# Block-sparse attention and a gated MLP on one core: the mask of 36 of 44 block pairs by eight products of 32 columns instead of two of 128

## The chip, the cores and the metric

The kernel runs on one core of one Trainium2 chip. The metric is the device time of one execution in microseconds. The engines named below are TensorE (PE, its weight loads shown apart as PEld), VectorE (DVE), ScalarE (ACT), GpSimd (POOL) and SyncE (SP).

## What is computed

Attention over 4 batches, 8 heads, 768 positions and a head size of 64, with a mask in blocks of 32 positions (24 blocks). A block of queries sees its neighbours, the first and the last block, and three sampled blocks; the first and the last block of queries see everything. The result goes through an MLP with 512 inputs, 2048 hidden units and 512 outputs.

```python
scores = scale * np.matmul(q, k.transpose(0, 1, 3, 2))
mask = np.abs(blk_i - blk_j) <= window
mask = mask | (blk_i == 0) | (blk_j == 0) | (blk_i == n_blocks - 1) | (blk_j == n_blocks - 1)
for qb in range(n_blocks):
    for kb in sampled_blocks[qb]:
        mask[qb * block:(qb + 1) * block, kb * block:(kb + 1) * block] = True
scores = np.where(mask, scores, -1000000000.0)
...
attn = attn / (np.sum(attn, axis=-1, keepdims=True) + 1e-09)
...
h = x @ w_in
g = h * (1.0 / (1.0 + np.exp(-beta * h)))
return (g @ w_out).astype(np.float32)
```

## The kernel before

The 22 inner query blocks of a batch are taken two at a time, which makes 11 pairs a batch and 44 pairs in all, numbered n = 0 to 43; p is the number within the batch. For a pair the kernel gathers eight key blocks for each of its two query blocks (three sampled, one and three fixed, one) into the tile KG, so that a row has 8 x 32 = 256 scores. The same sampled block can stand in the gathered row more than once, or beside a neighbour that is there already; such doubles are masked.

The scores of a pair lie in two PSUM banks, one for each head of a head pair (u = 0, 1). A bank holds 128 rows (four head pairs hp of 32 queries) by 512 columns (two query blocks g of 256). They are made by two steps that follow each other on PE:

- emit_sm, lines 810 to 818, writes the mask: a product of a constant tile `ones` (64 rows, 128 columns) with a small row of mask numbers `maskr`, spread over 32 columns a block. It covers `ns` = 3 blocks of each query block (192 columns in all), or 5 blocks (320 columns) for the first and the last pair of a batch (p = 0 and p = 10). One product for each bank, so two a pair. Each works on a PE tile of 64 rows by 128 columns.
- emit_ss, lines 820 to 830, adds the scores: sixteen products for a pair (g, hp, u), each on a PE tile of 64 rows by 32 columns, with 256 columns moving.

From pair 33 on, two pairs share one step of the order (lines 831 to 843): both masks first, then both sets of scores. These double steps are the pairs 34 and 35, 36 and 37, 38 and 39, 40 and 41, 42 and 43.

After that DVE takes the row maximum (L848), ACT the exponential (L856), DVE or POOL normalizes (L881), PE transposes (L895), ACT or DVE copies the transposes (L304, L306), and PE multiplies by V (L936, or L944 for the early pairs). The rows of the first and the last query block go through steps of their own (L1000 to L1063), and with 64x32 PE tiles for their scores (L1000). The MLP's products are L1129 (into the hidden layer, followed by a tanh on ACT at L1135 and a product on DVE at L1140) and L1156 (out of it). They are put between the attention steps all along.

The order of all steps is written out by hand in a long string ORDER; each engine runs its own steps in that order, and semaphores hold a step until its inputs are there. A step named sc7 in that string is the mask and the scores of pair 7, and a number behind a colon names PSUM banks. The string is the same for both kernels. Where it has two sc steps one behind the other (sc0, sc2 and sc1, for instance), PE goes from the scores of one pair straight to the mask of the next.

Of the kernel before, what the change touches and what calls it, by code (L numbers as in the profile page):

```python
# [192 lines left out]
def kernel(  # L193
# [11 lines left out]
    nc = tc.nc  # L205

    B, H, S, D = q.shape
    BLK = 32
# [3 lines left out]
    NHP = H // 2  # L212
# [12 lines left out]
    def sb(name, shape, dt=FP16):  # L225
        return pool.tile(shape, dt, name=name)
# [10 lines left out]
    NLATE, PTA, ODS, AHEAD = 11, 0.9, 0.8, 3  # L237
    NHOT, NV = 0, 2
    NHL, UP, NH32 = 4, 1024.0, 7

    by_dma = lambda n: n >= TD[0] and n % TD[1] < TD[2]
    TD = (31, 1, 1)
# [18 lines left out]
    ones = sb("ones", [P, P])  # L261
    maskr = sb("maskr", [P, NB - 2, 5])
# [389 lines left out]
    for n, (b, p) in enumerate(order_pairs):  # L652
# [157 lines left out]
        def emit_sm(n=n, p=p):  # L810
            bk = [bank(("S", n, u)) for u in range(2)]
            ns = 5 if p in (0, NPAIR - 1) else 3
            for u in range(2):
                nc.tensor.matmul(  # L814
                    bk[u][:, :].rearrange("x (g c) -> x g c", g=2)[:, :, 0:ns * BLK],
                    lhsT=ones[u * D:(u + 1) * D, :],
                    rhs=maskr[u * D:(u + 1) * D, 2 * p:2 * p + 2, 0:ns].to_broadcast([D, 2, ns, BLK]),
                    start=True, stop=False, skip_group_check=True, tile_position=(u * D, 0))

        def emit_ss(n=n, b=b, i0=i0, kgb=kgb):  # L820
            bk = [bank(("S", n, u)) for u in range(2)]
# [11 lines left out]
        if two == [n - 1]:  # L833

            t = sc[n] = sc[n - 1]
            t.deps += [d for d in sdeps if d not in t.deps]
            t.opens += (("S", n, 0), ("S", n, 1))
            t.ni *= 2
            halves[n - 1] += [emit_sm, emit_ss]
        else:  # L840
            halves[n] = [emit_sm, emit_ss]
            sc[n] = add(f"sc{n}", "PE", 0.62 if two else 0.31, lambda h=halves[n]: [f() for f in h[0::2] + h[1::2]],
                        deps=sdeps, prio=pr, lat=0.1, opens=(("S", n, 0), ("S", n, 1)))
# [388 lines left out]
```

## Time and profile before

| | us |
|---|---|
| median of 3 runs | 298.3 (297.95 to 299.88) |
| the profiled execution | 298.2 |
| its span, first to last instruction | 296.3 |
| PE busy | 277.1 |
| DVE busy | 227.2 |
| ACT busy | 220.4 |
| POOL busy | 170.1 |

The profile is of one execution. A row of the timeline or of the groups names an engine, a line of the kernel, the operation, what it writes and reads, the PE tile (rows x columns, written 64\*32), the size of the moving operand, and a count. The ends of products are modelled, so that a busy PE may be waiting for its own pipeline; what a product really costs is read from the starts. "Idle" is time in which an engine had nothing running.

### The profile page before, as it was taken

Reading aid. Unit: us, or ns where it says so; the run is one execution under the profiler, and the core shown is the slowest. Engines: PE = TensorE matmul, PEld = TensorE weight load, DVE = VectorE, ACT = ScalarE, POOL = GpSimd, SP = SyncE. Lnnn points to the kernel's source line nnn. Section 1 sums busy time; section 2 is a strip of 40 time slices with the busy share of each in tenths; the row PEclk is TensorE's granted clock in tenths of the full one; section 3 lists DMA queues with packets and bytes.
Section 4 is the critical chain, followed back from the end, with each engine's and each line's share of the span. In section 5 each row is a group of like instructions: output and inputs, shape, how many; then the busy total and the mean of one; then the engine's idle time right before and its main releaser. Section 6 shows DMA issues by size and latency. Waiting matters only on the chain.

```text
span 296.3 us, 10828 instructions
## 1 busy us (share of the span) xinstructions
PE 277.1 (94%) x3841; PEld 173.1 (58%) x3841; DVE 227.2 (77%) x538; ACT 220.4 (74%) x644; POOL 170.1 (57%) x508
## 2 busy tenths in 40 slices
PE   1599999898999999999999999999999999999993
PEld 0455768667577577655656665555455455557641
DVE  5879889987999899899998999787867642575420
ACT  3328989889999798979989989768758644855630
POOL 3058986316898997878777788748545606000000
PEclk9999999999999999999999999999999999999998
DMA  7999999999966745936973256355654554630203
GB/s 246 366 310 200 227 236 229 220 210 212 196 108 146 162 130 194 200 107 114 241 161 107 78 163 223 85 118 132 124 158 94 169 121 146 175 89 0 73 35 106
DMA packets 57168, 47.51 MB, mean 160 GB/s; under 512 B 19734, under 2 KB 53143, under 8 KB 57115
## 3 DMA queue, kind: packets, MB, share of 16 engines
q1 hardware_dynamic: 44736, 35.48, 41.8%
q0 software_dynamic: 12320, 11.27, 24.7%
q8 instruction: 30, 0.49, 0.7%
q14 instruction: 24, 0.19, 0.2%
q10 hardware_dynamic: 58, 0.07, 0.1%
HBM read 45.23 MB, written 9.44 MB: 184 GB/s over the span
## 4 chain that ended last, share of the span: by engine, by line
PE 69%; ACT 11%; DVE 11%; DMA 3%; issue 3%; SPq 0%; POOL 0%; DVEq 0%; ACTq 0%
PE bank L1156 24%; PE bank L1129 22%; ACT PP L856 5%; PE bank L936 4%; PE bank L791 4%; PE bank L825 4%; PE bank L895 3%; DVE g L1140 3%; DMA g<-in_k_dram 3%; PE bank L593 2%; ACT t L1135 2%; PE bank L814 2%; DVE ST L848 1%; ACT PG L1023 1%; PE bank L1043 1%
## 5 line engine op out<-in xcount | busy, mean ns | idle before, releaser
L1129 PE MATMUL bank<-xT,w_in_sb 128*128 128x256 f16 (+1 forms) x512 | 93.7, 326 | 1.0 <-DVE xT L960 0.4
L856 ACT ACTIVATE PP<-bank,ST 128x256 f16<-128x256 f32 x176 | 82.0, 484 | 16.2 <-DVE ST L848 7.6
L1156 PE MATMUL bank<-w_out_sb,g 128*128 128x512 f16 x384 | 90.6, 379 | 0.7 <-DVE xT L306 0.6
L1140 DVE SCALAR_TENSOR_TENSOR g<-t,bank 128x512 f16<-128x512 f16 (+1 forms) x128 | 67.1, 548 | 25.2 <-ACT t L1135 24.4
L1135 ACT ACTIVATE t<-bank,beta_sb 128x512 f16<-128x512 f32 (+1 forms) x128 | 70.9, 591 | 19.9 <-PE bank L1129 11.3
L881 POOL TENSOR_SCALAR PP<-PP,ST 128x256 f16<-128x256 f16 x132 | 63.7, 500 | 29.6 <-ACT PP L856 10.2
L1129 PEld LDWEIGHTS <-w_in_sb 128*128 128x128 f16 x512 | 54.5, 114 | 27.7 <-issue 3.8
L676 POOL COPY KG<-KT 128x64 f32 x264 | 52.4, 247 | 23.7 <-ACT KT L304 11.4
L848 DVE TENSOR_REDUCE ST<-bank 128x2 f32<-128x512 f32 x88 | 58.1, 681 | 5.8 <-PE bank L825 4.6
L1156 PEld LDWEIGHTS <-g 128*128 128x128 f16 x384 | 36.0, 98 | 39.8 <-issue 2.6
L856 ACT ACTIVATION_READ_ACCUMULATOR PP<-bank,ST 128x1 f32 x176 | 37.8, 215 | 0.0
L1035 POOL TENSOR_SCALAR PG<-PG,SG 128x768 f16<-128x768 f16 x14 | 12.6, 903 | 18.8 <-ACT t L1135 7.7
L310 ACT ACTIVATE osb<-bank 128x512 f32<-128x512 f32 (+1 forms) x24 | 14.0, 595 | 10.9 <-PE bank L1156 10.6
L1023 ACT ACTIVATE PG<-bank,SG 128x384 f16<-128x384 f32 x32 | 18.2, 583 | 2.4 <-DVE SG L1016 2.1
L936 PEld LDWEIGHTS <-VG 128*128 128x128 f16 x448 | 16.1, 98 | 5.0 <-issue 1.1
L895 PE MATMUL bank<-identity,PP 128*128 128x128 f16 x248 | 18.6, 219 | 0.4 <-ACT PP L856 0.2
L306 POOL COPY KG<-KT 128x384 f32<-128x384 f32 (+3 forms) x44 | 17.3, 419 | 1.7 <-PE bank L825 1.7
L895 PEld LDWEIGHTS <-PP 128*128 128x128 f16 x248 | 15.5, 98 | 4.6 <-issue 1.7
L306 DVE COPY PT<-bank 128x1024 f16<-128x1024 f16 x24 | 16.3, 682 | 1.8 <-PE bank L895 1.1
L306 DVE CAST xT<-bank 64x256 f16<-64x256 f32 (+1 forms) x33 | 13.6, 415 | 5.2 <-PE bank L936 4.7
L936 PE MATMUL bank<-PT,VG 128*128 128x64 f16 x448 | 17.2, 193 | 0.2 <-ACT PP L856 0.2
L825 PE MATMUL bank<-KG,QT 64*32 64x256 f16 x704 | 17.2, 274 | 0.0
(114 smaller groups left out, 304.4 us busy)
## 6 DMA issues: line engine op xcount, KB each, us to landing
VG<-VT SPq DMA_DIRECT2D x220, 32.0 KB, 2.2
VG<-VT SPq DMA_DIRECT2D x32, 192.0 KB, 2.8
out_dram<-osb SPq DMA_DIRECT2D x20, 256.0 KB, 2.3
RQ<-in_q_dram POOLq DMA_DIRECT2D x6, 384.0 KB, 9.2
RK<-in_k_dram POOLq DMA_DIRECT2D x6, 384.0 KB, 8.5
RV<-in_v_dram POOLq DMA_DIRECT2D x6, 384.0 KB, 8.6
VT<-Vn SPq DMA_DIRECT2D x3, 768.0 KB, 3.8
w_in_sb<-in_moe_w_in_dram POOLq DMA_DIRECT2D x8, 256.0 KB, 7.5
```

The costliest lines, as they stand in the source:

```text
L306: (nc.vector if eng == "DVE" else nc.gpsimd).tensor_copy(out=out, in_=in_)
L676: nc.gpsimd.tensor_copy(out=kg32[:, g, :, (SR + r) * W:(SR + r + 1) * W], in_=kt32[:, :, bass.ds(vals[3 * g + r], W)])
L825: nc.tensor.matmul(bk[u][hp * BLK:(hp + 1) * BLK, g * 256:(g + 1) * 256], lhsT=QT[b % 2][u * D:(u + 1) * D, hp, (i0 + g) * BLK:(i0 + g + 1 ...
L848: mx[n, u] = add(f"mx{n}.{u}", "DVE", 0.6, lambda n=n, u=u, sb_=sb_: nc.vector.tensor_reduce(out=sb_[:, 0, 2 * u:2 * u + 2], in_=bank(("S" ...
L856: nc.scalar.activation(out=pb[:, u, g, :], in_=bank(("S", n, u))[:, g * 256:(g + 1) * 256], func=AF.Exp, bias=sb_[:, 0, 2 * u + g:2 * u + ...
L881: (nc.vector if eng == "DVE" else nc.gpsimd).tensor_scalar(out=pb[:, u, g, :], in0=pb[:, u, g, :], scalar1=sb_[:, 2, 2 * u + g:2 * u + g + ...
L895: nc.tensor.transpose(out=o[:, s * P:(s + 1) * P], in_=pb[:, u, g, c * P:(c + 1) * P], identity=identity)
L936: nc.tensor.matmul(o[:, (g * NHP + hp) * 2 * BLK:(g * NHP + hp + 1) * 2 * BLK], lhsT=vgb[:, g, c, hp * P:(hp + 1) * P], rhs=pt[:, g, c, :, ...
L1129: nc.tensor.matmul(o[:, 0:TW], lhsT=w_in_v[:, c, f // 4, f % 4, :], rhs=xT[:, c, c0:c0 + TW], start=(c == 0), stop=(c == NHP - 1))
L1135: lambda G=G, f=f, TW=TW, tt=tt: nc.scalar.activation(out=tt[:, 0:TW], in_=bank(("H", G, f))[:, 0:TW], func=AF.Tanh, bias=0.0, scale=beta_ ...
L1140: lambda G=G, f=f, TW=TW, tt=tt, gg=gg: nc.vector.scalar_tensor_tensor(out=gg[:, f, 0:TW], in0=tt[:, 0:TW], scalar=1.0, in1=bank(("H", G, ...
L1156: nc.tensor.matmul(o[:, :], lhsT=gg[:, f, s * P:(s + 1) * P], rhs=w_out_sb[:, f, :], start=(f == 0), stop=(f == N_FFC - 1))
```

## The change

A set FEW names the pairs 3 to 10. For these the mask is written as before, by two products of 128 output columns. For all other pairs it is written by eight products with 32 output columns each, one for each head pair and bank, on the same 64x32 PE tiles and in the same hp, u order as the scores that follow. They read the same `maskr` and a part of the same `ones`, so the numbers that land in PSUM are the same.

```diff
+    FEW = range(3, 11)
...
-            for u in range(2):
-                nc.tensor.matmul(
-                    bk[u][:, :].rearrange("x (g c) -> x g c", g=2)[:, :, 0:ns * BLK],
-                    lhsT=ones[u * D:(u + 1) * D, :],
-                    rhs=maskr[u * D:(u + 1) * D, 2 * p:2 * p + 2, 0:ns].to_broadcast([D, 2, ns, BLK]),
-                    start=True, stop=False, skip_group_check=True, tile_position=(u * D, 0))
+            if n in FEW:
+                for u in range(2):
...
+                return
+            for hp in range(NHP):
+                for u in range(2):
+                    nc.tensor.matmul(
+                        bk[u][hp * BLK:(hp + 1) * BLK, :].rearrange(
+                            "x (g c) -> x g c", g=2)[:, :, 0:ns * BLK],
+                        lhsT=ones[u * D:(u + 1) * D, 0:BLK],
+                        rhs=maskr[u * D:(u + 1) * D, 2 * p:2 * p + 2, 0:ns].to_broadcast([D, 2, ns, BLK]),
+                        start=True, stop=False, skip_group_check=True,
+                        tile_position=(u * D, hp * BLK))
```

PE's instructions grow from 7572 to 8004: 36 pairs by six more products, each with its weight load. Leaving the mask aside, the order and the waits on every engine are the same in both kernels.

On PE, at the first pair of the kernel (n = 0), where its mask ends and its scores begin; the banks are numbered 122 and 124. Before:

```order
L814 LDWEIGHTS ones
L814 MATMUL bank_122<-maskr,ones 128x2x160
L814 LDWEIGHTS ones
L814 MATMUL bank_124<-maskr,ones 128x2x160
L825 LDWEIGHTS QT_74
L825 MATMUL bank_122<-KG_81,QT_74 32x256
L825 LDWEIGHTS QT_74
L825 MATMUL bank_124<-KG_81,QT_74 32x256
```

On PE at the same place, now (line 824 is the narrow mask, 837 the scores); the last two of the eight products are shown:

```order
L824 LDWEIGHTS ones
L824 MATMUL bank_122<-maskr,ones 32x2x160
L824 LDWEIGHTS ones
L824 MATMUL bank_124<-maskr,ones 32x2x160
L837 LDWEIGHTS QT_74
L837 MATMUL bank_122<-KG_81,QT_74 32x256
L837 LDWEIGHTS QT_74
L837 MATMUL bank_124<-KG_81,QT_74 32x256
```

The first number of a size is the count of output rows: 128 before, 32 now, so that mask and scores have the same PE tile.

On PE, where the scores of pair 0 end and the mask of the next pair in the order (n = 2) begins. Before:

```order
L825 LDWEIGHTS QT_74
L825 MATMUL bank_122<-KG_81,QT_74 32x256
L825 LDWEIGHTS QT_74
L825 MATMUL bank_124<-KG_81,QT_74 32x256
L814 LDWEIGHTS ones
L814 MATMUL bank_123<-maskr,ones 128x2x96
L814 LDWEIGHTS ones
L814 MATMUL bank_121<-maskr,ones 128x2x96
```

On PE at the same place, now:

```order
L837 LDWEIGHTS QT_74
L837 MATMUL bank_122<-KG_81,QT_74 32x256
L837 LDWEIGHTS QT_74
L837 MATMUL bank_124<-KG_81,QT_74 32x256
L824 LDWEIGHTS ones
L824 MATMUL bank_123<-maskr,ones 32x2x96
L824 LDWEIGHTS ones
L824 MATMUL bank_121<-maskr,ones 32x2x96
```

Here too the size of the tile no longer changes, where the mask follows on another pair's scores.

More of the change, by code (lines that the diff above doesn't have):

```diff
@@ L812, in emit_sm @@
             ns = 5 if p in (0, NPAIR - 1) else 3
-            for u in range(2):
-                nc.tensor.matmul(
-                    bk[u][:, :].rearrange("x (g c) -> x g c", g=2)[:, :, 0:ns * BLK],
-                    lhsT=ones[u * D:(u + 1) * D, :],
-                    rhs=maskr[u * D:(u + 1) * D, 2 * p:2 * p + 2, 0:ns].to_broadcast([D, 2, ns, BLK]),
-                    start=True, stop=False, skip_group_check=True, tile_position=(u * D, 0))
+            if n in FEW:
+                for u in range(2):
+                    nc.tensor.matmul(
+                        bk[u][:, :].rearrange("x (g c) -> x g c", g=2)[:, :, 0:ns * BLK],
+                        lhsT=ones[u * D:(u + 1) * D, :],
+                        rhs=maskr[u * D:(u + 1) * D, 2 * p:2 * p + 2, 0:ns].to_broadcast([D, 2, ns, BLK]),
+                        start=True, stop=False, skip_group_check=True, tile_position=(u * D, 0))
+                return
+            for hp in range(NHP):
+                for u in range(2):
+                    nc.tensor.matmul(
+                        bk[u][hp * BLK:(hp + 1) * BLK, :].rearrange(
+                            "x (g c) -> x g c", g=2)[:, :, 0:ns * BLK],
+                        lhsT=ones[u * D:(u + 1) * D, 0:BLK],
+                        rhs=maskr[u * D:(u + 1) * D, 2 * p:2 * p + 2, 0:ns].to_broadcast([D, 2, ns, BLK]),
+                        start=True, stop=False, skip_group_check=True,
+                        tile_position=(u * D, hp * BLK))
         def emit_ss(n=n, b=b, i0=i0, kgb=kgb):
```

## The prediction

> **What bounds the kernel now.** I read the page first, for the shares of the engines and of the chain of waits.
>
> ```profile
> PE 277.1 (94%) x3841; PEld 173.1 (58%) x3841; DVE 227.2 (77%) x538; ACT 220.4 (74%) x644; POOL 170.1 (57%) x508
> PE 69%; ACT 11%; DVE 11%; DMA 3%; issue 3%; SPq 0%; POOL 0%; DVEq 0%; ACTq 0%
> ```
>
> PE is busy for 94% of the span and holds 69% of the chain. But a mean hides the stages, so next I cut the span into windows: busy time of each engine and its count, the granted clock, the DMA share.
>
> ```profile
> 25.00:74.00 49.00, 45.62 (x907) 34.70 (x905) 43.41 (x118) 43.50 (x138) 31.80 (x91) 1.00 1.15 218
> 74.00:107.00 33.00, 32.42 (x623) 21.39 (x620) 30.23 (x73) 30.27 (x104) 29.80 (x87) 1.00 0.74 155
> 107.00:131.00 24.00, 23.99 (x370) 17.00 (x362) 22.44 (x55) 22.79 (x73) 19.79 (x68) 1.00 0.64 157
> 131.00:141.00 10.00, 9.79 (x186) 5.91 (x187) 9.38 (x21) 7.92 (x23) 8.38 (x16) 1.00 0.62 126
> 141.00:172.00 31.00, 31.00 (x463) 19.66 (x461) 28.29 (x62) 29.51 (x86) 23.65 (x65) 1.00 0.64 143
> 172.00:209.00 37.00, 37.00 (x445) 20.06 (x444) 30.36 (x71) 29.64 (x93) 26.96 (x87) 1.00 0.54 145
> 209.00:217.00 8.00, 6.91 (x82) 3.60 (x80) 7.09 (x14) 3.75 (x9) 3.29 (x11) 1.00 0.64 140
> 217.00:242.00 25.00, 25.00 (x271) 12.98 (x256) 14.66 (x28) 17.05 (x48) 11.68 (x38) 1.00 0.48 132
> ```
>
> Columns are PE, PEld, DVE, ACT, POOL. From 25 to 74 us PE is idle for 3.4 us, and DVE and ACT are busy for 43.4 and 43.5 of 49. From 107 to 172 PE is idle for 0.2 us of 65, but ACT works 60.2 and DVE 60.1 of them: three engines are nearly full, PE the fullest. From 172 to 209 and from 217 to 242 PE alone is full. Between, at 209 to 217, it waits for 1.1 us.
>
> The chain in order of time says the same of the stages; some of its pieces (start, length, what):
>
> ```profile
> 23.81 2.72 PE bank L791 x12
> 30.68 1.11 ACT PP L856 x5
> ...
> 121.73 3.58 PE bank L1129 x20
> ...
> 132.28 0.94 DVE SG L1014 x2
> ...
> 207.00 1.02 ACT PP L856 x4
> ```
>
> It runs on PE until 28 us, on ACT and DVE in turn with PE until 107, then mostly on PE, with detours over DVE and ACT at 131 to 140 and 206 to 216. So PE time that is saved is worth most from 107 us on, less between 25 and 107.
>
> **What a mask costs now.** The timeline of PE at pairs 21 and 20 shows it: the first has 320 columns, the second follows on the scores of the first and has 192.
>
> ```profile
> 120.55 0.31 PE L814 MATMUL bank<-maskr,ones 64*128 64x320 f16 x2
> 120.79 0.41 PE L825 MATMUL bank<-KG,QT 64*32 64x256 f16 x16
> 121.13 0.26 PE L814 MATMUL bank<-maskr,ones 64*128 64x192 f16 x2
> 121.32 0.41 PE L825 MATMUL bank<-KG,QT 64*32 64x256 f16 x16
> 121.66 0.73 PE L1129 MATMUL bank<-xT,w_in_sb 128*128 128x256 f16 x5
> ```
>
> By starts, a mask of 320 columns takes 0.24 us, one of 192 takes 0.19, and scores take 0.34 until work on another PE tile starts. Where the same tile size follows on scores, the trace has this case (scores of a pair, then L1000):
>
> ```profile
> 102.21 0.41 PE L825 MATMUL bank<-KG,QT 64*32 64x256 f16 x16
> 102.44 0.51 PE L1000 MATMUL bank<-KT,QT 64*32 64x384 f16 x16
> ```
>
> There the scores take 0.23 us. The change of tile size costs 0.11 us. A mask pays it on its way out, and once more on its way in where it stands behind another pair's scores.
>
> **What a narrow mask would cost.** No row of before shows one, so I bound it. Sixteen score products go in two waves of eight; the first eight alone, cut out by a short window, end at 0.30, all sixteen at 0.41:
>
> ```profile
> 22.34 0.30 PE L825 MATMUL bank<-KG,QT 64*32 64x256 f16 x8
> ...
> 102.44 0.35 PE L1000 MATMUL bank<-KT,QT 64*32 64x384 f16 x8
> ```
>
> So eight narrow products of 256 columns take 0.41 - 0.30 = 0.11 us, and eight of 384 columns 0.51 - 0.35 = 0.16. For a mask of 192 columns the low end is 0.11 x 192/256 = 0.08, the high end of this kind 0.11; I take 0.10, between them, since whether columns or weight loads set a wave is open at that size. For 320 columns I take 0.14, between 0.11 and 0.16. The far end is the row for products that do not run beside each other:
>
> ```profile
> 118.84 0.47 PE bank L936 x16
> ```
>
> 0.47/16 = 0.029 each, eight of them 0.23. It is far because L936 uses the whole array; the eight score products share it as the masks would. A gain below the 0.08 is excluded by the columns that must go through.
>
> A double step has four wide products for two pairs, then the scores:
>
> ```profile
> 194.82 0.34 PE L814 MATMUL bank<-maskr,ones 64*128 64x192 f16 x4
> 195.09 0.63 PE L825 MATMUL bank<-KG,QT 64*32 64x256 f16 x32
> ```
>
> 0.27 us now, two waves of 0.10 after.
>
> **The sum.** The masks lie in these stages (count of products, two a pair; 25 to 74 are the unchanged pairs 3 to 10):
>
> ```profile
> 20.00:25.00 5.00, 0.82 (x6) 0.29 (x6) 1.00 1.10 252
> 25.00:74.00 49.00, 2.11 (x16) 1.03 (x16) 1.00 1.15 218
> 74.00:107.00 33.00, 2.36 (x18) 0.86 (x18) 1.00 0.74 155
> 107.00:141.00 34.00, 1.90 (x14) 0.67 (x14) 1.00 0.63 147
> 141.00:172.00 31.00, 1.28 (x10) 0.48 (x10) 1.00 0.64 143
> 172.00:209.00 37.00, 1.30 (x12) 0.42 (x12) 1.00 0.54 145
> 209.00:242.00 33.00, 1.08 (x12) 0.43 (x12) 1.00 0.52 134
> ```
>
> Outside the double steps, ten of the changed masks stand right behind another pair's scores in the written order (pairs 2, 1, 12, 15, 20, 23, 26, 28, 30 and 33; all but 33 with 192 columns). Sixteen do not (0, 11, 21, 22 and 32 with 320 columns, eleven with 192).
>
> - Eleven with 192 columns: 0.19 - 0.10 = 0.09 each, 0.99 us.
> - Five with 320: 0.24 - 0.14 = 0.10, 0.50 us.
> - Nine behind scores: 0.09 and the 0.11 of the way in, 0.20, 1.80 us. Pair 33: 0.21.
> - Five double steps: 0.27 - 0.20 = 0.07, 0.35 us.
>
> Together 3.85 us of PE time. By stage: 0.50 (20 to 25), 1.04 (74 to 107), 0.98 (107 to 141), 0.67 (141 to 172), 0.45 (172 to 209), 0.21 (209 to 242).
>
> How much reaches the end is a choice, from the windows. The 0.50 must cross the stretch from 25 to 74 where ACT and DVE carry much of the chain: a third, 0.17. Of the 1.04 at 74 to 107, with PE idle 0.6 and the chain shared, half: 0.52. Of the 1.65 from 107 to 172, where PE has no idle time but ACT and DVE have under 8% to spare, three quarters: 1.24. Of the 0.45 before the detour at 206, four fifths, and all of the 0.21: 0.57. Sum 2.5 us. If the cover were complete, that is if ACT and DVE could follow at once, it would be all 3.85.
>
> The other edits cost nothing: no wait moves, no other engine has another instruction, and the six more weight loads a pair stand behind products of the same tile size, as those of the scores do.
>
> The profiled execution took 298.2 us, of which the span is 296.3; the median of the runs is 298.3. The difference of 0.1 is nothing here, and I count from 298.3: 295.8.
>
> **Rivals.**
>
> (a) Full effect: the chain from 12.5 us on touches PE again and again, and if the other engines shift with it, all 3.85 us come through: 294.4. For it speaks that PE is never idle at 141 to 209; against it that ACT is busy 29.5 of 31 at 141 to 172. Chance 0.20.
>
> (b) ACT and DVE take over as the bound until 172 us, and only the 0.57 of the late stages is left: 297.7. The windows speak for it, since their busy times leave out the gaps between instructions. Against it: then PE should show waits at 107 to 172 already, and it has 0.2 us. Chance 0.21.
>
> (c) The narrow products start one after another at the L936 spacing, 0.23 a mask. Then single masks of 192 columns lose 0.04 each (0.44), those of 320 gain 0.01 (0.05), those behind scores gain 0.07 (0.63), pair 33 gains 0.12, and the double steps lose 0.19 each (0.95): 0.6 us of PE time more, 298.7 at the same share of 2.5/3.85. Against it: the first eight score products end within 0.30 us, and all have started before the window's end, 0.08 after the first. The Trainium skill, "TensorE: Matmul & The Clock Gate", section "Wait — 56ns, not 53.3ns?", says that starts of matmuls never come closer than about 25 ns; as an estimate by that page a mask would take 0.20 us, and the sum would fall from 3.85 to about 0.5 us. By that floor eight starts would spread over 0.18 us, and the trace has them within 0.08. Chance 0.08.
>
> (d) Slower: PE's code arrives late. The page has
>
> ```profile
> q8 instruction: 30, 0.49, 0.7%
> ```
>
> (packets, MB, share), and 7682 products and weight loads over 30 packets make 256 instructions a packet, 16 KB. The change adds 432 instructions, 1.7 packets, all outside 25 to 74 us, where the DMA share is 1.15. But 36 of them stand ahead of that stretch and move every later packet's border, and each following stretch gets denser (74 to 107: 1243 rows now, 108 more). PE's longest wait of this kind, with no releaser, is
>
> ```profile
> PE bank L944 <- issue: 0.4, 1, 0.4
> ```
>
> From 74 to 242 us run some 4850 rows, 19 packets. If each border cost 0.4, that is 7.6 us, less the 2.5 gained: 303.4. It decides from 2.5/19 = 0.13 us a border. Against it: with the same borders PE shows only this one such wait, and the densest stretch gets no instruction of its own. The Trainium skill, "Runtime: NRT & Kernel Launch", section "Instruction fetch mechanics", says that the next block of 256 instructions is fetched while the current one runs, and that a border is mostly hidden; by it this rival costs nothing. The 256 a packet agree with it. Chance 0.08.
>
> **The numbers.** The forecast, 295.8 with a range of its own from 295.0 to 296.7, has 0.43. The range for 8 in 10 goes from 294.2 (full effect, and the runs' scatter) to 298.7 (c); it leaves out (d) and the edge of (a). A change within 1%, 3.0 us, is about what a measurement of this kernel can tell from none. Faster by more, below 295.3: (a) with 0.20 and a third of the forecast, 0.35. Slower by more, over 301.3: most of (d), 0.06. Within: 0.59.
>
> **What would show it.** In the profile after: a narrow mask of 192 columns 0.08 to 0.11 us ahead of its scores (0.23 would be c); scores that last 0.23 us where a mask follows; PE's time from 107 to 242 us shorter by some 2 us with idle time still near zero (more idle, with ACT and DVE fuller, would be b); no new waits without releaser on PE (d). The prediction is wrong if a narrow mask costs as much as a wide one, or if PE at 107 to 172 waits for as much as it saves.

## The result, and the profile after

| | before | changed kernel |
|---|---|---|
| median, 20 runs each | 298.02 us | 297.25 us |
| ratio to before | | 0.9961, 95% interval 0.9942 to 0.9979 |
| profiled execution, span | 298.2, 296.3 us | 296.95, 295.1 us |
| PE busy in the span | 277.1 us | 273.6 us |

The change gains 0.4%, some 1.2 us by the ratio: in the direction of the forecast and inside its range, but half of the 2.5 us that were forecast. The ratios here and below leave disturbed runs out and the medians do not, so that the two can differ (three of 20 runs of the changed kernel are left out, and three of seven of the kernel with all masks narrow).

The page of the changed kernel (busy time of each engine; then the chain that ended last, by engine):

```profile
PE 273.6 (93%) x4057; PEld 173.9 (59%) x4057; DVE 226.3 (77%) x538; ACT 220.6 (75%) x644; POOL 170.0 (58%) x508
PE 60%; DVE 12%; DMA 10%; ACT 9%; issue 3%; POOL 2%; POOLq 1%; SPq 1%; DVEq 0%; ACTq 0%
```

PE has 216 more products and is busy for 3.5 us less. Its share of the chain fell from 69% to 60%. The masks do what was worked out. The timeline of PE at pairs 21 and 20 of the changed kernel (start, length, what; L824 is the narrow mask, L837 the scores):

```profile
114.73 0.33 PE L824 MATMUL bank<-maskr,ones 64*32 64x320 f16 x8
114.87 0.40 PE L837 MATMUL bank<-KG,QT 64*32 64x256 f16 x16
115.09 0.27 PE L824 MATMUL bank<-maskr,ones 64*32 64x192 f16 x8
115.17 0.40 PE L837 MATMUL bank<-KG,QT 64*32 64x256 f16 x16
115.51 0.30 PE L1141 MATMUL bank<-xT,w_in_sb 128*128 128x256 f16 x1
```

By starts: a mask of 320 columns 0.14 us (0.24 before), scores with a mask behind them 0.22 (0.34), a mask of 192 columns 0.08 (0.19). At three of the ten places where a mask follows on scores, these take 0.31 to 0.39 us and not 0.22. (The rows that the prediction quoted for the wide masks belong to the pairs 22 and 23, not 21 and 20; they have the same two shapes.) Added up over all masks by these starts, the PE time that is saved is a little over the 3.85 us of the sum, and 1.2 arrive.

How far the changed kernel is ahead can be read where the same mask starts in both traces, one of each kernel:

| mask of pair | before, us | changed kernel | ahead |
|---|---|---|---|
| 0 | 22.10 | 21.68 | 0.42 |
| 11 | 74.95 | 75.12 | -0.17 |
| 17 | 97.15 | 96.49 | 0.66 |
| 18 | 102.03 | 101.97 | 0.06 |
| 19 | 106.46 | 106.30 | 0.16 |
| 26 | 139.01 | 138.50 | 0.51 |
| 32 | 178.35 | 177.59 | 0.76 |
| 42 | 240.75 | 239.54 | 1.21 |

The 0.42 us ahead of the first mask are no work of the change. The lead is lost up to pair 11, comes back, is lost once more between the pairs 17 and 18, and then grows by 1.05 us up to pair 42, where the sum has some 2.3.

Where the rest went after 107 us shows in the chain. Before, it ran on PE from 114 to 131 us. In the changed kernel, some of its pieces there:

```profile
113.50 0.86 PE bank L1168 x4
115.35 1.89 DVE ST L860 x3
117.23 0.74 DVE g L1152 x2
...
121.25 0.59 DVE ST L860
...
125.22 0.69 DVE g L1152
125.91 0.60 DVE ST L860
...
129.38 1.17 DVE g L1152 x2
```

The stretch has changed hands: after the pairs 21 and 20, on which PE saves 0.33 us, DVE's row maxima (L860) and its MLP product (L1152) are what ended last. The same can be read at single waits. The first product with V behind the pairs 26 and 25, before:

```profile
140.34 0.42 PE L936 MATMUL bank<-PT,VG 128*128 128x64 f16 x9 [0.20 <-ACT PP L856]
```

and in the changed kernel, where the two masks ahead of it are narrow:

```profile
139.83 0.54 PE L948 MATMUL bank<-PT,VG 128*128 128x64 f16 x13 [0.43 <-ACT PP L868]
```

The wait for ACT grew from 0.20 to 0.43 us. From the start of pair 26's mask (in the table) to this product it takes 1.33 us in both kernels: all that the two pairs gained, 0.23 us, is handed back at once.

A second loss, earlier, is of another kind. The timeline of PE in the changed kernel between the pairs 17 and 18:

```profile
96.49 0.28 PE L824 MATMUL bank<-maskr,ones 64*32 64x192 f16 x8
96.58 0.40 PE L837 MATMUL bank<-KG,QT 64*32 64x256 f16 x16
96.91 0.49 PE L956 MATMUL bank<-PT,VG 128*64 128x32 f16 x20
98.64 0.43 PE L956 MATMUL bank<-PT,VG 128*64 128x32 f16 x17 [1.24 <-issue]
```

PE stops for 1.24 us in the middle of a run of equal products, with no releaser. It stops after 3264 instructions of its trace, 192 + 256 x 12, which is a border of its code packets. It fits the late code of the prediction's rival (d), though not in full: a packet landed at 97.4 us, where the wait begins, and the trace does not show what fills the 1.2 us after that. The same trace has a second such wait, at instruction 961, where the kernel before waits 0.41 us:

```profile
40.38 0.44 PE L931 MATMUL bank<-idf,HLF 128*64 128x128 f32 x4 [0.88 <-issue]
```

After 107 us no PE wait without releaser of over 0.2 us stands in any trace of this case.

### The profile page after: what moved, and what is told of

The parts are those of the page before. It is cut to its first block, busy times and chain, and to the rows that moved or that the text cites. A ratio compares the mean times of both kernels' runs of the same rounds, so it can differ in the third digit from the quotient of the medians.

```text
span 295.1 us, 11260 instructions
## 1 busy us (share of the span) xinstructions
PE 273.6 (93%) x4057; PEld 173.9 (59%) x4057; DVE 226.3 (77%) x538; ACT 220.6 (75%) x644; POOL 170.0 (58%) x508
## 4 chain that ended last, share of the span: by engine, by line
PE 60%; DVE 12%; DMA 10%; ACT 9%; issue 3%; POOL 2%; POOLq 1%; SPq 1%; DVEq 0%; ACTq 0%
PE bank L1168 24%; PE bank L1141 21%; DVE g L1152 4%; PE bank L948 4%; ACT PP L868 4%; DMA w_in_sb<-in_moe_w_in_dram 3%; PE bank L907 3%; ACT t L1147 3%; DMA VT<-Vn 2%; DVE ST L860 2%; DMA xT<-in_v_dram 2%; DMA VG<-VT 2%; PE bank L837 2%; PE bank L824 2%; PE bank L594 1%
## 5 line engine op out<-in xcount | busy, mean ns | idle before, releaser
L1152 DVE SCALAR_TENSOR_TENSOR g<-t,bank 128x512 f16<-128x512 f16 (+1 forms) x128 | 67.0, 548 | 25.7 <-ACT t L1147 25.0
L860 DVE TENSOR_REDUCE ST<-bank 128x2 f32<-128x512 f32 x88 | 58.1, 680 | 4.6 <-PE bank L837 3.1
L837 PE MATMUL bank<-KG,QT 64*32 64x256 f16 x704 | 16.5, 270 | 0.2
```

Of the source, the lines that this page charges most:

```text
L837: nc.tensor.matmul(bk[u][hp * BLK:(hp + 1) * BLK, g * 256:(g + 1) * 256], lhsT=QT[b % 2][u * D:(u + 1) * D, hp, (i0 + g) * BLK:(i0 + g + 1 ...
L860: mx[n, u] = add(f"mx{n}.{u}", "DVE", 0.6, lambda n=n, u=u, sb_=sb_: nc.vector.tensor_reduce(out=sb_[:, 0, 2 * u:2 * u + 2], in_=bank(("S" ...
L1152: lambda G=G, f=f, TW=TW, tt=tt, gg=gg: nc.vector.scalar_tensor_tensor(out=gg[:, f, 0:TW], in0=tt[:, 0:TW], scalar=1.0, in1=bank(("H", G, ...
```

## The experiments

Three theories. **A**: the gain was eaten by late code, and depends on where the borders of PE's code packets lie. **A2**: PE's saved time is given back because DVE, ACT and POOL are close behind it, whatever the code does. **B**: a fixed share arrives, without a place. PE time below is counted with the prediction's figures. The kernel before had medians of 298.3 to 298.5 us beside these runs.

### Which pairs: five other choices

Each is one line of the changed kernel.

```diff
-    FEW = range(3, 11)
+    FEW = range(0, 20)                                              # e1_wide_0_19
+    FEW = ()                                                        # e2_narrow_all
+    FEW = range(0, 11)                                              # e6_wide_0_10
+    FEW = [n for n in range(44) if n not in (12, 15, 20, 23, 26, 28, 30, 33)]   # e7_followers
+    FEW = [*range(0, 11), *range(16, 20)]                           # e10_wide_0_10_16_19
```

> Pairs 0 to 19 keep the wide mask, only 20 to 43 get the narrow one. Theory A (late code): up to 107 us PE's code is as before, so the borders of its 256-instruction packets lie on the same work as before and no new late packet can come; the later masks are worth what they gave in the changed kernel from 102 us on, 1.1 us: 296.9, and no PE wait without releaser above 0.5 us. Theory B (no code effect; DVE and ACT simply absorb a fixed share, 0.8 of 3.85 us): this kernel saves 2.3 us of PE time, so 0.5 us: 297.5.

> All 44 pairs get the narrow mask. It saves PE another 8 x 0.1 = 0.8 us and puts 96 more instructions into the stretch from 28 to 63 us. Theory A (late code): PE waits of over 1 us in all without releaser appear between 28 and 75 us, each at an instruction number of 193 + 256k; the time is 297.8 or more, slower than the changed kernel. Theory B (no code effect): 297.1, a little faster than the changed kernel.

> Pairs 0 to 10 wide, 11 to 43 narrow: the borders of PE's code up to 75 us lie as in the kernel before, and only the first three pairs' gain (0.5 us of PE time) is given up. Theory A (the early gain is lost anyway to the weights that land at 42 us, and the changed kernel paid for a late border at 98.6 us): 0.8 us gained from 74 to 98 us and 1.1 from 107 on: 296.4 to 296.8 if before is 298.3, at least as fast as the changed kernel. Rival (the gain is spread evenly, a quarter of the PE time saved): 297.5, slower than the changed kernel.

> Only the pairs 12, 15, 20, 23, 26, 28, 30 and 33, whose mask stands right behind another pair's scores, get the narrow mask: 1.6 us of PE time for 96 instructions, against 3.35 us for 396 instructions from pair 11 on in the changed kernel. Theory A2 (share of PE time): 0.35 from the two early ones, and a bit under half of the 1.2 us of the late ones: 0.9 us less than before, 297.4 if before is 298.3, with no more scatter than before. Rival (late code is what costs): nearly all of the 1.6: 296.7.

> Narrow masks for the pairs 11 to 15 and 20 to 43 only; the pairs 16 to 19, in the stretch around the late border at 98.6 us, stay wide. 3.0 us of PE time, 348 instructions. Theory A: from 74 to 98 us most of the 0.7 us of PE time is kept and no border there is late, from 107 us on 1.1 us: 1.7 us under before, 296.6 if before is 298.3, the fastest of the versions. Theory B (no code effect): 0.3 of 3.0, 297.4.

| narrow pairs | PE time saved | median | ratio to before, interval | gain by the ratio |
|---|---|---|---|---|
| all but 3 to 10 (the change) | 3.85 us | 297.25 | 0.9961 (0.9942 to 0.9979) | 1.2 us |
| 20 to 43 | 2.31 | 297.41 | 0.9976 (0.9952 to 0.9999) | 0.7 |
| all | 4.65 | 298.31 | 0.9944 (0.9922 to 0.9966) | 1.7 |
| 11 to 43 | 3.35 | 297.40 | 0.9960 (0.9937 to 0.9982) | 1.2 |
| 12, 15, 20, 23, 26, 28, 30, 33 | 1.5 | 297.84 | 0.9966 (0.9944 to 0.9989) | 1.0 |
| 11 to 15, 20 to 43 | 3.0 | 297.81 | 0.9962 (0.9929 to 0.9994) | 1.1 |

The fifth line saves 1.5 us of PE time and not the 1.6 of its expectation: in the written order pair 25 stands behind pair 26, not 26 behind 25, so that seven of its eight masks stand right behind other scores. (The prediction's list has the same slip; its count of ten is right.)

Theory A did badly by the times. All narrow, with 96 more instructions in the stretch where the DMA queues are full, should have been slower than the changed kernel; its ratio, which rests on four runs, is the lowest of this table, though its median over all seven, 298.31 us, is what A expected. The waits that A expected there do stand in its trace, which is of an execution of 301.9 us: 0.97 us at 39.6 and 1.56 at 58.0 us, both without releaser. The choice that keeps code away from the late border has no such wait near 98 us in its trace, and gained no more than the change. Five of the six lines lie near a third of the PE time saved, as B and A2 have it; the fifth line lies at two thirds, close to the 0.9 us that A2 expected of it. The intervals, of 0.4 to 0.7% in width, don't tell these versions from one another. In the traces of the second and the last line PE also waits 1.0 and 0.8 us near 246 us for a transfer of transposes, which it does neither before nor in the changed kernel; so what comes close behind PE is not DVE and ACT alone.

The profile of the second line has a lesson of its own. Up to 107 us its code is instruction for instruction that of before. Near 40 us, at a border of code packets, the kernel before waits

```profile
40.63 0.46 PE L944 MATMUL bank<-PT,VG 128*64 128x32 f16 x18 [0.41 <-issue]
```

and this one

```profile
41.02 0.46 PE L956 MATMUL bank<-PT,VG 128*64 128x32 f16 x18 [1.24 <-issue]
```

The same code at the same border waits 0.8 us longer, from one execution to another kernel's. One trace can't say what such a wait costs in the mean. But eight traces have this border on the same work. In four it held PE for 0.4 to 0.6 us, and these executions lie within some 0.3 us of their kernels' medians; in four it held PE for 1.2 to 1.4 us, and these lie 0.6 us or more above them. That the wait makes the difference is not shown; in these eight it goes with it.

### The borders of the code moved, with nothing else changed

Tiny products at the front, where PE waits for its inputs until 10 us, shift every border. For 64 instructions in the changed kernel, and 36, 120 and 256 in the kernel before (the last two in two and three portions):

```diff
     def emit_fill(k, i):
         for _ in range(k):
-            nc.tensor.matmul(banks[i][:, 0:256], lhsT=heat, rhs=heat[:, :].rearrange(
-                "x (a m) -> x a m", a=1).to_broadcast([P, 2, P]), start=True, stop=True, skip_group_check=True)
+            nc.tensor.matmul(banks[i][0:BLK, 0:8], lhsT=ones[:, 0:BLK], rhs=ones[:, 0:8],
+                             start=True, stop=True, skip_group_check=True)
...
-sbl ident ldV0.0 ...
+sbl ident fill32:7 ldV0.0 ...
```

> The changed kernel with 32 tiny products (64 instructions) put at the very front of PE, where PE waits for 10 us anyway; they move the borders of PE's code packets by 64 instructions and change nothing else. Theory A: the 1.4 us wait of PE at 98.6 us (instruction 3265 of its trace) goes, since the border then lies elsewhere; the stretch of code around it takes 6.3 us instead of 4.2 between the two borders: 296.3, about 0.9 under the changed kernel, unless another border becomes late. Theory B: 297.25, as the changed kernel.

> The kernel before with 18 tiny products (36 instructions) at the front of PE, where it waits anyway: the borders of the code packets up to 75 us then lie where the changed kernel has them, with no mask changed. Theory A: the time changes though no useful work does; PE's wait at the border near 40 us (instruction 961 of its trace) grows from 0.4 to 1 us, as in the changed kernel: 298.3 to 298.8. Theory B: 298.0.

> The kernel before with 128 tiny products (256 instructions) in PE's idle time ahead of 10 us: the borders of the code packets lie on the same work as before, one packet later. Theory A (what counts is where the borders lie): no change, within 0.3 us of before. Rival (the tiny products themselves cost): seven times as many as in the shift by 36, so at least the 0.7 us that this one cost, likely 1 to 3 us.

> The kernel before with 60 tiny products (120 instructions) in the same idle time. By the trace of before, the time between a border and the next then is under 5 us at six borders from 58 to 107 us, against none without the shift and two or three with a shift by 36. Theory A: slower than the shift by 36, 1 to 2 us over before, with PE waits without releaser of over 1 us in the trace. Rival: between the shift by 36 and the shift by 256.

| kernel | shift | median | ratio to before, interval |
|---|---|---|---|
| changed | 64 | 297.49 us | 0.9976 (0.9943 to 1.0010) |
| before | 36 | 299.16 | 1.0030 (1.0011 to 1.0048) |
| before | 120 | 299.45 | 1.0021 (0.9994 to 1.0048) |
| before | 256 | 299.70 | 1.0039 (1.0016 to 1.0062) |

In the changed kernel the shift by 64 removed the wait at 98.6 us, as A expected: its trace has no PE wait without releaser of over 0.2 us. The time did not fall, 297.49 us against 297.25. The shift by 36 looked like a success for A: slower, as expected; but in its trace the wait near 40 us, which was to grow to 1 us, is 0.3. The shift by 256 is the control, and A fails there: the borders lie on the same work as before, and it is as slow as the others. The shift by 120, which should have been the worst, is not. So the tiny products cost 0.6 to 1.2 us by the ratios however the borders lie, and the intervals don't show that the cost grows with their number. In the trace of the shift by 256 PE loses time at two places: its second run of K transposes, at 12.55 us before, starts at 13.70, since it waits 1.77 us for DVE where before waited 0.76; and at the border near 40 us it waits

```profile
42.22 0.46 PE L944 MATMUL bank<-PT,VG 128*64 128x32 f16 x18 [1.39 <-issue]
```

where before waited 0.41. Why is not settled. These shifts give no support to the theory that a border's place decides the time. They don't exclude it for the wait at 98.6 us either, since the tiny products cost about what A expected to gain there. That PE waits at some borders stays as the traces show it.

### PE time taken away and added without the code

If A2 holds, the gain must be lost too when PE's time is saved without new instructions. The kernel before without the mask of pairs 20 to 43 (the doubled blocks of these pairs are then not masked):

```diff
         def emit_sm(n=n, p=p):
+            if n >= 20:
+                return
...
-                            start=False, stop=True, skip_group_check=True,
+                            start=n >= 20, stop=True, skip_group_check=True,
```

> The kernel before without any mask for pairs 20 to 43 (so their outputs lack the mask of doubled blocks): no code is added, PE loses 0.19 us for each single pair, 0.30 where it stood behind another pair's scores, 0.27 for a double step, 4.9 us in all, nearly all of it after 107 us. Theory A2 (from 107 us on DVE, ACT and POOL take over as soon as PE runs ahead; a bit under half of the saved PE time arrives, as in the changed kernel, where 1.1 of 2.3 us did): 2.3 us less than before, 296.0 if before is 298.3. Rival (PE alone sets the end there, and what was lost in the changed kernel was lost to late code): nearly all of it, 293.6.

Measured: 296.35 us, ratio 0.9932 (0.9906 to 0.9958), 2.0 us of 4.9, with an interval from 1.2 to 2.8. A2 expected 2.3, its rival 4.9. With 96 instructions fewer than before, and no PE wait without releaser behind the one near 40 us, late code is no explanation. At the same product as above the wait for ACT is longer still:

```profile
139.73 0.65 PE L938 MATMUL bank<-PT,VG 128*128 128x64 f16 x16 [0.51 <-ACT PP L858]
```

In the other direction, the wide mask of pairs 20 to 43 written twice:

```diff
-            for u in range(2):
+            for u in (0, 1) * (2 if n >= 20 else 1):
                 nc.tensor.matmul(
```

> The kernel before with the wide mask written twice (the same values) for pairs 20 to 43: 0.09 us of PE time more for each of 24 pairs, 2.2 us (0.15 for the three with 320 columns, so 2.4), and 96 instructions more after 107 us. Theory A2 (DVE, ACT and POOL are close behind PE; PE is still the fullest engine there): most of it arrives, 1.5 to 2.4 us slower, so that the time answers to PE time more than it did when PE got faster (0.41 of it). Rival (the engines share the bound evenly): the same share of 0.4 in this direction, 1.0 us slower.

Measured: 300.15 us, ratio 1.0051 (1.0029 to 1.0074), 1.5 us slower of 2.2 to 2.4 added: a share of 0.65, against 0.41 when PE got faster. The intervals overlap (0.9 to 2.2 us here), so the times alone don't show that the two directions differ. The trace does at this place: the wait for ACT is gone.

```profile
140.49 0.60 PE L936 MATMUL bank<-PT,VG 128*128 128x64 f16 x15
```

So at one product, PE's wait went 0, 0.20, 0.43, 0.51 us as PE's work ahead of it grew shorter. The other traces repeat it: 0.19 to 0.21 us in the three shifts of the kernel before, 0.43 in every other kernel with both masks narrow, 0.30 in the one where only the first of the two is.

### DVE made lighter

If DVE is what PE now waits for, less work on DVE must gain time, with PE untouched. In the changed kernel, the row maximum of pairs 20 to 43 over 128 of 256 scores of a row. The other half is left out of the maximum; a softmax does not need the exact maximum as long as the scores are small, which holds for these inputs and is no property of the method.

```diff
-                in_=bank(("S", n, u))[:, :].rearrange("x (g c) -> x g c", g=2),
+                in_=bank(("S", n, u))[:, :].rearrange("x (g c) -> x g c", g=2)[:, :, 0:128 if n >= 20 else 256],
```

> The changed kernel, whose row maximum (L860) for pairs 20 to 43 is taken over 128 of a row's 256 scores (half of the maximum is left out; the softmax still holds as long as the scores are small). It takes roughly 0.25 us from each of 48 reductions on VectorE, 12 us in all, and changes nothing on PE. Theory A2 (from 107 us on PE's saved time is given back because DVE, and POOL and ACT behind it, deliver late): the PE waits near 139.8 and 179.5 us shrink, and the 1.2 us that PE gave back after 107 us return wholly or in great part: 1.0 to 1.5 under the changed kernel, 295.8 to 296.3. Rival (what PE waits for is ACT's own exponential chain or a DMA): the time stays at 297.2.

Measured: 295.63 us, ratio 0.9901 (0.9870 to 0.9932), the fastest of all kernels here: 3.0 us under before, 1.8 under the changed kernel, somewhat more than A2 expected. The row maxima by shape, of the changed kernel and of this one (shortest, median and longest, ns):

```profile
L860 DVE TENSOR_REDUCE ST<-bank x88: 658/680/692, 22.4 to 243.1; 128x2 f32<-128x512 f32 x88
```

```profile
L860 DVE TENSOR_REDUCE ST<-bank x88: 392/425/693, 23.1 to 241.1; 128x2 f32<-128x256 f32 x48, 128x2 f32<-128x512 f32 x40
```

Some 0.26 us less for each of 48. Windows of both (columns PE, PEld, DVE, ACT, POOL), first the changed kernel:

```profile
107.00:131.00 24.00, 23.94 (x420) 17.35 (x416) 22.32 (x55) 22.79 (x72) 19.71 (x68) 1.00 0.67 164
141.00:172.00 31.00, 30.90 (x489) 19.83 (x488) 28.59 (x63) 29.71 (x87) 23.79 (x67) 1.00 0.63 144
```

```profile
107.00:131.00 24.00, 23.95 (x408) 17.13 (x403) 20.72 (x56) 22.44 (x71) 19.65 (x69) 1.00 0.65 163
141.00:172.00 31.00, 30.86 (x493) 19.81 (x492) 25.62 (x63) 29.68 (x88) 24.43 (x70) 1.00 0.58 135
```

DVE drops by 1.6 and 3.0 us, ACT nearly stays. The chain goes back to PE. Its pieces that touch 107 to 141 us, added up by engine (us):

| kernel | PE | DVE | ACT |
|---|---|---|---|
| before | 25.3 | 1.8 | 5.9 |
| before, mask of pairs 20 to 43 twice | 34.0 | 0 | 0 |
| changed | 7.8 | 14.2 | 10.4 |
| changed, lighter maxima | 24.1 | 1.1 | 7.7 |

Code does not explain the gain: the wait at the border near 98 us, 1.24 us, is there in this trace too. One place where the time returns is a run of eight hidden-layer products behind the pairs 32 and 33 (before, changed, lighter DVE):

```profile
179.99 1.97 PE L1129 MATMUL bank<-xT,w_in_sb 128*128 128x512 f16 x8
```

```profile
178.90 2.19 PE L1141 MATMUL bank<-xT,w_in_sb 128*128 128x512 f16 x8
```

```profile
177.76 1.93 PE L1141 MATMUL bank<-xT,w_in_sb 128*128 128x512 f16 x8
```

The 0.22 us that the run grew by in the changed kernel are gone. What the run waits for is named in the kernel without the late masks, where its fifth product waits 0.27 us for ACT's exponential, which itself follows on DVE's maximum:

```profile
180.06 1.02 PE L1131 MATMUL bank<-xT,w_in_sb 128*128 128x512 f16 x4 [0.27 <-ACT PP L858]
```

The wait at the product with V, which was expected to shrink as well, stays as it was; DVE's maxima don't set that one:

```profile
138.83 0.63 PE L948 MATMUL bank<-PT,VG 128*128 128x64 f16 x16 [0.43 <-ACT PP L868]
```

What lighter maxima alone would do to the kernel before was not tried. So it is shown that DVE's work held the changed kernel back after 107 us; how much of the 1.8 us is the masks' lost time, and how much the kernel before would gain as well, is not.

## Why the prediction came out as it did

**PE's saving: right.** A narrow mask of 192 columns takes 0.08 us where 0.10 was taken, one of 320 columns 0.14 as taken, scores with a mask behind them 0.22 for 0.23 at seven places of ten. The way in and out between tile sizes, 0.11 us, is paid only where the neighbour has another tile. Rival (c), products that start one after another, is out: eight products of 192 columns and the first scores' start lie within 0.08 us. The floor of 25 ns between starts that the Trainium skill gives ("TensorE: Matmul & The Clock Gate", section "Wait — 56ns, not 53.3ns?") does not hold for products on tiles that work side by side.

**The share that arrives: mis-sized.** This is the term that failed. The prediction let 2.5 of 3.85 us come through, with three quarters of the part from 107 to 172 us, 1.24, and four fifths or all of it later, 0.57. What arrived in all is 1.2 us. By the table of starts the lead grew by 0.60 us from pair 19 to pair 32, and by 0.45 from there to pair 42. So the share from 107 to 172 us is the term that was furthest off, at half of its size. PE's time from there to 242 us was to be shorter by some 2 us; it is shorter by 1.05. Where PE time was saved without new code, after 107 us, 0.41 of it arrived. Rival (b), DVE and ACT as the next bound, had the mechanism; its price of 0.6 us was too low for a gain of 1.2, as the forecast's 2.5 was too high. The prediction's argument against (b), that PE should then show waits already, was wrong: an engine can be without idle time and still have another one only tenths behind it. PE's idle time before was 0.2 us from 107 to 172, and the chain passed to DVE where PE had saved 0.33 us.

**The early pairs: no gain, where little was expected, and for another reason too.** The prediction gave the first three pairs a third of 0.5 us. Set against before product by product, the changed kernel's PE is 1.0 us ahead at 24 us and 0.5 behind at 48. One cause in this trace is the wait of 0.88 us at 40.4 us, and its waits name another:

```profile
PE bank L1141 <- DMA w_in_sb<-in_moe_w_in_dram: 0.5, 1, 0.5
```

The first hidden-layer products wait for their weights. The kernel that leaves these pairs wide has the same ratio within the noise, 0.9960.

**Late code, rival (d): present, its price open.** It did not make the kernel slower, as (d) had it, and it is not what was lost after 107 us. Ahead of that, one border costs PE 1.24 us at 98.6 us; the lead falls by 0.60 between the pairs 17 and 18, so that the next waits take about half of it back. Up to there all that the masks of the pairs 11 to 16 saved, 0.77 us by the sum, had come through: the lead grew by 0.83. The prediction took half of 1.04 for the whole stretch; what was left at pair 19 is 0.33. This is read from one trace of each kernel. The Trainium skill's page "Runtime: NRT & Kernel Launch", section "Instruction fetch mechanics", has the borders mostly hidden; most are, and these traces have waits of 0.2 to 1.6 us at a few of them. The experiments on border places failed their own control, and the choices with less code were not faster. What makes a border late in one execution and not in another stays open, and so does the wider scatter of the changed kernel (its lowest run is 294.3 us, 2.9 under its median; that of before 297.6, 0.5 under).

## What to carry to other kernels

Before crediting time saved on the fullest engine, look at the second and third: where they are busy for over 90% of the same stretch, as here from 107 to 172 us, about two fifths of PE's saving arrived, and taking work from the second engine gained time with PE untouched. Idle time near zero on the first engine does not say how close the next one is; a wait that is already there, however short, is a place to look: here the one of 0.20 us took back the whole gain of the two pairs ahead of it. A shift experiment needs its control: a shift by a whole period, which must change nothing.

## What the runs showed of the hardware

- Eight products on 64x32 tiles run side by side also when they are only 192 columns wide: 0.08 us for the eight, so that splitting a wide product into eight costs nothing here and spares the change of tile size.
- Small products in PE's idle time at the start, 18 to 128 of them, cost 0.6 to 1.2 us at the end by the ratios (the interval of the 60 reaches to no cost), the 128 only 0.3 us more than the 18, which is within the noise.
- The code border near 40 us held PE for 0.41 us in one trace and 1.24 in another with the very same code ahead of it; over eight traces with this work at the border, 0.4 to 1.4 us.
